# Chunked attention and a squared-ReLU feed-forward layer: where three blocks' transposes of x are done

## The chip, the cores and the metric

One core of a Trainium2 chip runs the kernel. The metric is the device time of one execution in microseconds (us); 283.85 us is the median of three executions before the change.

The engines are named as the profile names them: PE (TensorE: matrix products, and PEld, its weight loads), DVE (VectorE), ACT (ScalarE), POOL (GpSimd) and SP (SyncE, which here issues DMAs). Each engine has its own instruction queue, which it works off in the order in which the program put instructions in it.

## The reference

The inputs q, k and v have 8 batches, 8 heads, 576 positions and 64 elements a head. Attention stays inside chunks of 64 positions. Its output, 4608 rows of 512, goes through a feed-forward layer with 2048 hidden units:

```python
scores = scale * np.matmul(q_c, k_c.transpose(0, 1, 2, 4, 3))   # 64 x 64 per chunk and head
attn = softmax(scores)
x = matmul(attn, v_c)             # -> rows of 512
h = np.maximum(x @ w_in, 0.0)
return (h * h @ w_out).astype(np.float32)
```

## The kernel before

**Tiling.** A group is 256 rows (four chunks); there are 18. A block is two groups, 512 rows; there are 9, numbered 0 to 8. Groups 14 and 15 (block 7) consist of the four leftover chunks of four batches each; all others have four neighbouring chunks of one batch.

**What is done for a group g.** Its q and k are loaded by SP, cast to bf16 (`C`, on ACT or POOL) and transposed into `qkT` (`TD`, a DMA transpose on SP). `SC` (`scores`, L474) makes the scores in PSUM, and ACT takes the exponential `e` (L485). `AV` (`values`, L501) multiplies by v in two halves, `AV0` and `AV1`; after each half DVE takes a reciprocal (L435) and multiplies (L436), which gives half of `x`. `XT` (`transpose_x`) turns x into `xT`, the form that the feed-forward layer reads. It has two ways: eight PE transposes into one PSUM tile (L531) and a copy of 128x1024 out of it by ACT (L536), or one DMA transpose from SBUF to SBUF issued by SP (L526). `FIRST_DMA_X = 12` gives the DMA way to groups 12 to 17, which are blocks 6, 7 and 8.

**PSUM.** SC, each half of AV, and XT by PE each take a tile from `att_bank()`. In blocks 0 to 3 two tiles, `ps_att` and `ps_att2`, are given out in turn. From block 4 on there is `ps_att` alone. So such a step can write only when the reader of the tile's last content (ACT's exponential or copy, DVE's multiply) is done.

**The order is written by hand in slots.** While block j is worked on, attention for block j+1 and loads, casts and `qkT` for block j+2 are placed between its pieces.

Block 2: slots 0 to 15 follow the sixteen pieces of `ffn_in` (four products of 128x512 each, then a ReLU on ACT, L581, and a square into `gT`, L588). At slots 14 and 15 DVE is also given the sums of gT that the output stage needs (`g_sum`, L604): at 14 the first half of `d4`; at 15 the second half of d4, then d5, d3 and d2, seven additions. Slots 16 to 18 come with no work of the block. Slots 19 to 32 follow the fourteen half products of the output stage (`ffn_out`, L766), eight matrix products each. The seven products read, in this order: gT alone; d4; d5; d3; gT; gT; d2. They accumulate in two PSUM tiles, and after the second (slot 22), third and fourth, ACT copies a tile to `kept` (L823). The third product adds to the tile that the copy of slot 22 reads.

Blocks 4 to 8 use a fast form of the first product with seven smaller products, on four quarters ("ticks") of four slots. A slot s of such a block runs in this order: its `quad_step`s (L647: eight matrix products, or four in every fourth slot), what was placed at s - 0.5, half a product of the output stage of the block before (L766, eight matrix products; in block 4 in some slots only, and in blocks 5 to 8 at 0, 2, 3 and 5 to 15), and what was placed at s. From block 5's on, SC, AV0, AV1 and XT of the next block's two groups are placed by `S0`, `V0`, `V1` and `X0`. The four sums `e1` to `e4` of xT (`x_sums`, L604 `qk_st<-xT`), which the next block's first slots read, are placed at 13.5, 15, 17.5 and 18. e1 needs the first group's xT, e2 the second's. e1 is read in the next block's slot 0, e2 in its slot 2, e3 in its slot 3.

In the quad steps ACT copies one result (L683, L689, L692) or takes a ReLU (L703), DVE adds and clips (L655), and the squares go to ACT (L664), DVE and POOL (L666), some steps later.

Of the kernel before, what the change touches and what calls it, by code (L numbers as in the profile page):

```python
# [144 lines left out]
def kernel(  # L145
# [34 lines left out]


    FIRST_DMA_T = 4
    FIRST_DMA_X = 12
    QUADS = 4
    LEAD = 4

# [128 lines left out]
    def go(pieces):  # L315
        for f in pieces:
            f()
# [24 lines left out]
    def half_of(g):  # L342

        return g % 2 if g // 2 < QUADS else 1 - g % 2

    def x_tile(j):
        if j not in xTs:
            xTs[j] = att_pool.tile([128, BT // 128, n_dt, 128], BF16, name="xT", bufs=2)
        return xTs[j]
# [171 lines left out]
    def transpose_x(g):  # L521
        x = state.pop(("x", g))
        n = 2 * half_of(g)
        dst = x_tile(g // 2)[:, n:n + 2].rearrange("p t h q -> p (t h) q")
        if g >= FIRST_DMA_X:
            nc.sync.dma_start_transpose(out=dst, in_=x.rearrange("p t h a d -> p (t h a d)"))  # L526
            return
        psb = att_bank().bitcast(BF16)[:, 0:1024].rearrange("p (b q) -> p b q", q=128)
        for t in range(2):
            for hp in range(n_hp):  # L530
                nc.tensor.transpose(  # L531
                    out=psb[:, t * n_hp + hp, :],
                    in_=x[:, t, hp].rearrange("p a d -> p (a d)"),
                    identity=ident)
        copy = nc.vector.tensor_copy if g == blocks[1][0] else nc.scalar.copy
        copy(out=dst, in_=psb)  # L536
# [372 lines left out]
    def pieces(grps):  # L909
        for g in grps:  # L910
            yield from qk_pieces(g)
        for g in grps:
            yield from v_pieces(g)

    SC, AV, XT = scores, values, transpose_x
    TD = transpose_qk_dma
# [67 lines left out]
    for j in range(QUADS):  # L984
        grps, nxt, far = blocks[j], blocks[j + 1], blocks[j + 2]
        plan = {}

        def at(slot, f, *x):
            plan.setdefault(slot, []).append((f, x))

        if j == 0:
            loads, go_slots = pieces(far), range(17)
            at(28, summed(b11_p_b21, b11, b21))
            for slot, f in ((24, TA), (27, SC), (29, AV), (31, XT)):
                at(slot, f, nxt[0])
            at(31, TQ, nxt[1])
            at(31, summed(b22_m_b21, b22, b21, ALU.subtract))
            phases = [first_ffn_in, ffn_out_by_ft(0)]
        elif j == 1:
            loads, go_slots = itertools.chain(*map(qk_pieces, far)), range(26, 48)  # L1000
            for slot, f in ((1, TK), (4, SC), (7, AV), (12, XT)):
                at(slot, f, grps[1])
            for i, g in enumerate(nxt):
                for slot, f in ((16 + 4 * i, C), (21 + 4 * i, TD), (36 + i, SC), (38 + 2 * i, AV),
                                (41 + 2 * i, XT)):
                    at(slot, f, g)
            for i, g in enumerate(far):
                at(36 + 4 * i, C, g)
                at(42 + 3 * i, TD, g)
            at(2, summed(b12_p_b21, b12, b21))  # L1010
            at(12, summed(b11_m_b12, b11, b12, ALU.subtract))
            at(20, summed(b12_p_b22, b12, b22))
            out_j = ffn_out(1)
            for i in (20, 27, 29, 31):
                at(i, lambda: next(out_j)())
            phases = [ffn_in(1, [(0, 256, FT_ORDER), (256, 256, FT_ORDER)]), out_j]
        else:
            out_j = ffn_out(j)
            for i in (14, 15):
                at(i, lambda: next(out_j)())  # L1020
            phases = [ffn_in(j, [(0, BT, range(n_ft))])]
            if j == 2:
                loads, go_slots = itertools.chain(*map(v_pieces, nxt), pieces(far)), [
                    *range(16), *range(27, 36)]
                slots = {SC: (6, 9), AV: (11, 15), XT: (14, 24), C: (21, 26), TD: (25, 29)}
                for f in (C, TD):
                    for i, g in enumerate(far):
                        at(slots[f][i], f, g)
                phases.append(out_j)
            else:  # L1030
                loads, go_slots = pieces(far), range(11)
                for f, slots in ((C, (11, 13)), (TD, (13, 15))):
                    for i, g in enumerate(far):
                        at(slots[i], f, g)
                slots = {SC: (2, 4), AV: (7, 10), XT: (13, 15)}
            for f in (SC, AV, XT):
                for i, g in enumerate(nxt):
                    at(slots[f][i], f, g)
            if j == 2:
                for i, f in enumerate((summed(a21_p_a22, a21, a22),  # L1040
                                       summed(a12_m_a21, a12, a21, ALU.subtract),
                                       summed(a11_p_a21, a11, a21))):
                    at(1 + 2 * i, f)
        slot = 0
        for phase in phases:
            for _ in phase:
                if slot in go_slots:
                    for f in loads:
                        f()
                        break  # L1050
                for f, x in plan.get(slot, []):
                    f(*x)
                slot += 1
        assert all(x < slot for x in plan), (j, slot, sorted(plan))
        if j < QUADS - 1:
            go(loads)
# [19 lines left out]
    for j in range(QUADS, n_blk):  # L1076
        if j == QUADS:
            n = 14 - LEAD
            slots = [1 + 19 * i // n for i in range(n)]
            assert len(slots) == n  # L1080
        else:
            slots = [s for s in range(4, 20) if s % 16 not in NO_OUT]
            start = 3
        if j == QUADS:
            between = {}
            for n in (0, 1, 2, 3):
                between.setdefault(n, []).append((load, (1, loads)))
            for n in (2, 2, 2, 3):
                between.setdefault(n, []).append((x_sums, (QUADS, len([1 for z in between.values() for y in z if y[0] is x_sums]))))
            for f, x in between.get(0, []):  # L1090
                f(*x)
            for i in range(LEAD):
                next(out_j)
                tock()
                for f, x in between.get(i + 1, []):
                    f(*x)
        else:
            outs[j - 1] = ffn_out(j - 1)
            at(j, start, lambda j=j: next(outs[j - 1])())
        for s in slots:  # L1100
            plan.setdefault(("out", 16 * (j - QUADS) + s), []).append(outs[j - 1])

        if j + 1 < n_blk:
            S0, V0, V1, X0 = ((1.5, 3.5), (4.5, 7.5), (6, 9.5), (8.5, 11.5)) if j == QUADS else (
                (0.5, 7), (2, 8), (3.5, 9.5), (3.5, 10)) if is_whole(blocks[j + 1][0]) else (
                (3.5, 9), (5, 10), (7, 11.5), (7.5, 12))
            for i, g in enumerate(blocks[j + 1]):
                at(j, S0[i], SC, g)
                at(j, V0[i], AV0, g)
                at(j, V1[i], AV1, g)  # L1110
                at(j, X0[i], XT, g)
            if j + 2 == n_blk:
                at(j, 22, check_sums)
                at(j, 25.5, count_bad)
            for i, s in enumerate((13.5, 15, 17.5, 18)):
                at(j, s, x_sums, j + 1, i)
        if j == QUADS:
            for s in range(4):
                at(j, 4 * s + 2, w_sums_in_place, s)
            assert next(loads, None) is None  # L1120
        if j + 2 < n_blk:
            more = pieces(blocks[j + 2])
            if j == n_blk - 3:

                for s, n in ((0, 1), (1, 1), (2, 1), (3, 1), (4, 1), (5, 1), (10, 2), (12.5, 3),
                             (14, 1), (14.5, 1), (15, 1), (15.5, 1)):
                    at(j, s, load, n, more)
            else:
                for s in range(0, 16):
                    at(j, s, load, 1 if is_whole(blocks[j + 2][0]) else 2, more)  # L1130
            for i in range(2):
                at(j, (9, 13)[i], C, blocks[j + 2][i])
                at(j, ((9.5, 13.5) if j == n_blk - 3 else (12, 13.5))[i], TD, blocks[j + 2][i])
# [66 lines left out]
```

## Time and profile before

| What | us |
|---|---|
| runs before: median (lowest to highest of 3) | 283.85 (282.85 to 285.76) |
| the profiled execution's own time | 284.43 |
| its span, first to last instruction | 282.7 |
| PE busy | 267.3 (95%) |
| DVE busy | 199.3 (71%) |
| ACT busy | 166.2 (59%) |
| POOL busy | 93.5 (33%) |

The page's first part gives these shares. The chain of work that ended last is followed back from the last instruction to what released each step. The view of waits says for how long an engine sat idle before a line and what ended that. In the timeline a row is: start, duration, engine, line, operation, result and operands, count, and in square brackets the idle time before it with its releaser. The granted clock of PE was 1.000 throughout.

Where the blocks lie in this execution: block 2 from 81.4 to 112.4 us, block 3 to about 132, block 4 to about 155, block 5 to about 181, block 6 to 208, block 7 from 208.45. PE's idle time is 6.0 us in the first 20 us, 4.2 us in the last 16.7, and 5.1 us between.

### The profile page before, as it was taken

To read this page: it belongs to the slowest core of one execution; us is meant where nothing else is said; L and a number is where in the kernel's file an instruction comes from. 1 tells how busy PE (TensorE), PEld (TensorE's weight loads), DVE (VectorE), ACT (ScalarE), POOL (GpSimd) and SP (SyncE) were. 2 spreads that over 40 slices of the span, in tenths; PEclk is the share of its full clock that TensorE was granted. 3 is DMA by queue.
4 is the path that set the end of the run, shared out by engine and by line. 5 is a ranking of instruction groups with operands and counts; after the bars stand their busy time and mean duration, and the time that the engine had idled before them with its cause. 6 is when DMAs were issued, how large, how long until landed. Compare 5 with 4: busy or idle time off the path is not lost.

```text
span 282.7 us, 7975 instructions
## 1 busy us (share of the span) xinstructions
PE 267.3 (95%) x3288; PEld 204.7 (72%) x3291; DVE 199.3 (71%) x367; ACT 166.2 (59%) x296; POOL 93.5 (33%) x123
## 2 busy tenths in 40 slices
PE   2999999999999989999999999999988999999994
PEld 2774455788764478457879888888866888888883
DVE  1277515999438491499989997889739977994751
ACT  1537614794468845866678766475656664656330
POOL 2047842440350003151245234541703322431612
PEclk9999999999999999999999999999999999999999
DMA  7999999989999994999998997598999420220323
GB/s 221 255 339 392 379 306 277 334 184 163 303 188 234 240 199 102 268 257 187 242 231 181 176 220 198 118 217 224 219 186 228 101 72 4 82 67 9 79 71 114
DMA packets 135480, 55.61 MB, mean 197 GB/s; under 512 B 104272, under 2 KB 131152, under 8 KB 135440
## 3 DMA queue, kind: packets, MB, share of 16 engines
q1 hardware_dynamic: 132432, 45.76, 70.7%
q0 software_dynamic: 2864, 9.18, 10.3%
q8 instruction: 27, 0.44, 0.7%
q10 hardware_dynamic: 144, 0.13, 0.1%
q14 instruction: 13, 0.11, 0.1%
HBM read 36.70 MB, written 9.44 MB: 163 GB/s over the span
## 4 chain that ended last, share of the span: by engine, by line
PE 76%; DMA 10%; DVE 8%; ACT 2%; issue 1%; SPq 1%; DVEq 0%; ACTq 0%
PE ps_ffn L647 19%; PE ps_out L766 18%; PE ps_ffn L570 14%; PE ps_ffn L766 11%; PE ps_ffn L883 5%; DMA xT<-x 4%; DMA qk_st<-in_k_dram 4%; DVE w_st L604 2%; PE ps_att L474 2%; PE ps_att L501 2%; DVE gT L588 2%; DMA qkT<-qkb 2%; DVE x L436 2%; PE ps_ffn L426 1%; PE ps_att L531 1%
## 5 line engine op out<-in xcount | busy, mean ns | idle before, releaser
L570 PE MATMUL ps_ffn<-xT,w_in_bf 128*128 128x512 bf16 (+1 forms) x328 | 58.7, 333 | 0.3 <-DVE xT L536 0.2
L766 PEld LDWEIGHTS <-w_st 128*128 128x128 bf16 x512 | 49.0, 98 | 7.3 <-issue 0.8
L655 DVE CUSTOM_DVE_ANT_0 relu<-ps_ffn,w_st 128x512 f32<-128x512 f32 x60 | 39.3, 684 | 12.9 <-PE ps_ffn L647 11.9
L588 DVE TENSOR_TENSOR gT<-relu 128x256 bf16<-128x256 bf16 (+2 forms) x69 | 33.3, 512 | 20.1 <-ACT relu L581 19.9
L581 ACT ACTIVATE relu<-ps_ffn 128x256 bf16<-128x256 f32 (+2 forms) x82 | 39.9, 504 | 11.7 <-PE ps_ffn L570 10.3
L570 PEld LDWEIGHTS <-w_in_bf 128*128 128x128 bf16 x328 | 30.9, 98 | 21.6 <-DVE xT L536 0.4
L795 POOL DMA_DIRECT2D out_dram<-o_sb x27 | 19.8, 732 | 52.3 <-DVE o_sb L604 50.9
L647 PE MATMUL ps_ffn<-qk_st,w_in_bf 128*128 128x256 bf16 x240 | 35.3, 273 | 1.2 <-DVE qk_st L604 1.2
L647 PEld LDWEIGHTS <-w_in_bf 128*128 128x128 bf16 x320 | 30.6, 98 | 5.6 <-DVE qk_st L604 1.0
L766 PE MATMUL ps_out<-w_out_bf,w_st 128*128 128x256 bf16 x240 | 31.0, 273 | 0.1
L766 PEld LDWEIGHTS <-gT 128*128 128x128 bf16 x296 | 28.5, 98 | 3.4
L689 ACT ACTIVATE w_st<-ps_ffn 128x512 f32<-128x512 f32 x20 | 11.9, 597 | 26.8 <-PE ps_ffn L647 26.8
L436 DVE TENSOR_TENSOR x<-ps_att,recs 128x512 bf16<-128x512 f32 x36 | 24.9, 691 | 1.2
L647 PEld LDWEIGHTS <-qk_st 128*128 128x128 bf16 x240 | 22.6, 98 | 4.3 <-DVE qk_st L604 1.4
L485 ACT ACTIVATE e<-ps_att 128x1024 bf16<-128x1024 f32 x18 | 18.4, 1024 | 11.8 <-PE ps_att L474 11.8
L666 POOL TENSOR_TENSOR qk_st<-relu 128x512 bf16<-128x512 f32 x10 | 10.3, 1034 | 41.9 <-DVE relu L655 41.9
L647 PE MATMUL ps_ffn<-xT,qk_st 128*128 128x256 bf16 x160 | 23.9, 273 | 0.0
L666 POOL TENSOR_TENSOR gT<-relu 128x512 bf16<-128x512 f32 x10 | 10.3, 1033 | 39.5 <-DVE relu L655 35.8
L442 POOL CAST qkb<-qk_st 128x1024 bf16<-128x1024 f32 x12 | 13.5, 1124 | 14.1 <-DMA qk_st<-in_q_dram 14.1
L664 ACT ACTIVATE gT<-relu 128x512 bf16<-128x512 f32 x28 | 17.7, 633 | 0.0
L766 PE MATMUL ps_ffn<-w_out_bf,w_st 128*128 128x256 bf16 x144 | 17.5, 273 | 0.0
L445 POOL CAST qkb<-qk_st 128x1024 bf16<-128x1024 f32 x12 | 14.6, 1215 | 8.4 <-DMA qk_st<-in_k_dram 8.4
(91 smaller groups left out, 433.7 us busy)
## 6 DMA issues: line engine op xcount, KB each, us to landing
qk_st<-in_q_dram SPq DMA_DIRECT2D x16, 512.0 KB, 5.4
out_dram<-o_sb POOLq DMA_DIRECT2D x31, 256.0 KB, 4.3
qk_st<-in_k_dram SPq DMA_DIRECT2D x24, 256.0 KB, 5.3
ve_sb<-in_v_dram SPq DMA_DIRECT2D x32, 128.0 KB, 3.9
w_st<-in_moe_w_in_dram SPq DMA_DIRECT2D x8, 512.0 KB, 6.4
w_st<-in_moe_w_out_dram SPq DMA_DIRECT2D x8, 512.0 KB, 5.5
vo_sb<-in_v_dram SPq DMA_DIRECT2D x24, 128.0 KB, 3.3
qk_st<-in_k_dram SPq DMA_DIRECT2D x4, 512.0 KB, 5.8
```

Of the source, the lines that this page charges most:

```text
L436: nc.vector.tensor_tensor(out=x, in0=o[:, :, :, 0:D], in1=rec.to_broadcast([128, 2, n, D]), op=ALU.mult)
L445: copies[1](out=qkb[:, 1], in_=loaded(g, 1))
L485: nc.scalar.activation(out=e_out, in_=s_in, func=AF.Exp, scale=scale)
L570: nc.tensor.matmul(out=h[:, 0:n], lhsT=w_in_bf[:, dt, ft * 128:(ft + 1) * 128], rhs=xT[:, c // 128:(c + n) // 128, dt, :], start=(dt == 0) ...
L581: nc.scalar.activation(out=rl[:, 0:n], in_=h[:, 0:n], func=AF.Relu)
L588: nc.vector.tensor_tensor(out=dst, in0=src, in1=src, op=ALU.mult)
L647: nc.tensor.matmul(out=bank[:, f * GT:(f + 1) * GT], lhsT=a[:, dt, ft * 128:(ft + 1) * 128], rhs=b[:, :, dt, :], start=(first and f == 0 a ...
L655: nc.vector._custom_dve(TENSOR_ADD_SAT, out=out, in0=in0, in1=in1, s0=BIG, s1=0.0)
L664: engine.activation(out=dst, in_=r, func=AF.Square)
L666: engine.tensor_tensor(out=dst, in0=r, in1=r, op=ALU.mult)
L766: nc.tensor.matmul(out=out_ps, lhsT=lhsT, rhs=b[:, i, :], start=(first and i == 0 and (last or t == 0)), stop=(i == HF - 1), skip_group_ch ...
L795: dma.dma_start(out=out[t0:t0 + GT, col:col + HD].rearrange("(t p) d -> p t d", p=128), in_=o_sb.rearrange("p (t d) -> p t d", d=HD))
```

## The change

Three edits.

1. The DMA way of XT is given to blocks 6 and 8 by name. Groups 14 and 15 (block 7) so take the PE way: sixteen PE transposes and two ACT copies in place of two DMA transposes. For the attention of block 7, placed during block 6, the slots of the first group's XT go from 7.5 to 8.5, and those of the second group from 9, 10, 11.5 and 12 (SC, AV0, AV1, XT) to 9.5, 10.5, 12 and 13.5.
2. In block 2, AV of group 7 goes from slot 15 to 14, and XT of groups 6 and 7 from slots 14 and 24 to 22 and 28.
3. In block 4, XT of group 10 goes from 8.5 to 8.

```diff
-    FIRST_DMA_X = 12
+    X_BY_DMA = (6, 8)
...
-        if g >= FIRST_DMA_X:
+        if g // 2 in X_BY_DMA:
             nc.sync.dma_start_transpose(out=dst, in_=x.rearrange("p t h a d -> p (t h a d)"))
             return
...
-                slots = {SC: (6, 9), AV: (11, 15), XT: (14, 24), C: (21, 26), TD: (25, 29)}
+                slots = {SC: (6, 9), AV: (11, 14), XT: (22, 28), C: (21, 26), TD: (25, 29)}
...
-            S0, V0, V1, X0 = ((1.5, 3.5), (4.5, 7.5), (6, 9.5), (8.5, 11.5)) if j == QUADS else (
+            S0, V0, V1, X0 = ((1.5, 3.5), (4.5, 7.5), (6, 9.5), (8, 11.5)) if j == QUADS else (
                 (0.5, 7), (2, 8), (3.5, 9.5), (3.5, 10)) if is_whole(blocks[j + 1][0]) else (
-                (3.5, 9), (5, 10), (7, 11.5), (7.5, 12))
+                (3.5, 9.5), (5, 10.5), (7, 12), (8.5, 13.5))
```

## The prediction, made before the change was run

> **What bounds the kernel now.** I read the shares first, then the chain that ended last.
>
> ```profile
> PE 267.3 (95%) x3288; PEld 204.7 (72%) x3291; DVE 199.3 (71%) x367; ACT 166.2 (59%) x296; POOL 93.5 (33%) x123
> ...
> PE 76%; DMA 10%; DVE 8%; ACT 2%; issue 1%; SPq 1%; DVEq 0%; ACTq 0%
> ```
>
> PE is busy nearly all the time, so a stage has to give what PE idles in it, and work added to PE costs its length. Of 15.4 us idle, 5.1 lie between the first 20 and the last 16.7 us. The view of PE's waits says on whom:
>
> ```profile
> PE ps_ffn L647 <- DVE qk_st L604: 2.4, 3, 1.3
> PE ps_att L501 <- ACT xT L536: 0.9, 2, 0.7
> PE ps_ffn L766 <- ACT kept L823: 0.7, 1, 0.7
> ...
> PE ps_att L531 <- DVE x L436: 0.2, 1, 0.2
> ```
>
> (Total, times, longest.) The first row stands for the sums of block 7's x; the others lie mostly in block 2. The chain shows the two DMA transposes of block 7's x, and the timeline what follows each:
>
> ```profile
> 199.56 8.38 DMA xT<-x
> ...
> 208.55 3.77 DMA xT<-x
> ```
>
> ```profile
> 207.96 0.43 DVE L604 TENSOR_TENSOR qk_st<-xT 128x512 bf16<-128x512 bf16 x1 [1.83 <-DMA xT<-x]
> ...
> 208.45 0.61 PE L647 MATMUL ps_ffn<-qk_st,w_in_bf 128*128 128x256 bf16 x4 [0.77 <-DVE qk_st L604]
> ...
> 212.42 0.42 DVE L604 TENSOR_TENSOR qk_st<-qk_st,xT 128x512 bf16<-128x512 bf16 x1 [3.43 <-DMA xT<-x]
> ...
> 212.90 0.61 PE L647 MATMUL ps_ffn<-qk_st,qk_st 128*128 128x256 bf16 x4 [1.28 <-DVE qk_st L604]
> ...
> 215.62 0.60 PE L647 MATMUL ps_ffn<-qk_st,w_in_bf 128*128 128x256 bf16 x4 [0.40 <-DVE qk_st L604]
> ```
>
> The transfers land late, DVE stands in front of e1 and e2, and PE behind DVE.
>
> **Edit 1 (block 6).** *Removed:* 0.77 + 1.28 + 0.40 = 2.45 us of PE waits. The first group's x is done at 194.4; PE reaches slot 8.5 at 195.83; ACT, idle from 194.97 to 197.30, copies (1.01 us) until 197.5, ten us ahead of e1. The second group's copy ends near 208.5 in my layout, e2's addition (0.42) near 209; PE needs it at 212.4.
>
> *Added on PE:* block 4's sets of eight transposes hold PE from 145.89 to 146.35 and from 150.06 to 150.51, so two sets cost 0.92. Nothing hides them.
>
> *Added wait:* the second group's SC now comes behind slot 10's quad steps, AV0 behind slot 11's. Counted from slot 10's first product, SC ends at 0.89 + 0.37 = 1.26, and PE stands at AV0 after an output half (0.96) and four products (0.44) more, at 2.66. ACT has three instructions ahead of the exponential that used to run behind it:
>
> ```profile
> 197.30 1.02 ACT L485 ACTIVATE e<-ps_att 128x1024 bf16<-128x1024 f32 x1 [2.34 <-PE ps_att L474]
> 198.22 0.59 ACT L689 ACTIVATE w_st<-ps_ffn 128x512 f32<-128x512 f32 x1
> 198.70 0.63 ACT L664 ACTIVATE gT<-relu 128x512 bf16<-128x512 f32 x1
> 199.22 0.60 ACT L703 ACTIVATE relu<-ps_ffn 128x512 f32<-128x512 f32 x1
> ```
>
> They start 0.5 apart; the first can start 0.63 after slot 10's first product (in slot 14: 204.46 and 205.09). So the exponential runs from 2.11 to 3.13, and PE waits some 0.5 us; behind AV0 on PE stand output products, which nobody else holds up. Bounds: 0 if the ACT work is out of the way, 1.02 if a whole exponential is waited for. I take 0.5.
>
> *On SP:* two issues (2.27 and 1.24 us) go. The cast that the next `qkT` transpose of SP needs ends at 200.6, and that transpose was issued at 201.92, behind the removed one; it and the v loads come earlier. The last v for AV0 of group 16 landed at 211.2 + 3.1 = 214.3, PE came at 214.90 and will come near 213.9; SP's head start of over 2 us covers that.
>
> Sum of edit 1: -2.45 + 0.92 + 0.5 = -1.0 (bounds -1.5 and -0.5).
>
> **Edit 2 (block 2).** PE's three waits there:
>
> ```profile
> 98.24 0.22 PE L501 MATMUL ps_att<-ve_sb,e 64*64 64x65 bf16 x2 [0.70 <-ACT xT L536]
> ...
> 102.84 1.91 PE L766 MATMUL ps_ffn<-w_out_sum,w_st 128*128 128x256 bf16 x16 [0.67 <-ACT kept L823]
> ...
> 105.22 0.40 PE L531 MATMUL ps_att<-ident,x 128*128 128x128 bf16 x4 [0.25 <-DVE x L436]
> ```
>
> Before, from the end of the last `ffn_in` piece (97.2) to block 3's first product (112.4) lie AV of group 7 with its wait, 1.29; seven products, 12.3; the `kept` wait, 0.67; group 7's XT with its wait, 0.87.
>
> After: AV takes the place of group 6's XT ahead of the last piece, at about the same PE time; its half of the PSUM tile is free when DVE's x ends at 95.96, as it was for XT. The 1.29 goes. Group 6's XT (0.46) fits into the `kept` wait (0.67), which stays as a whole. Group 7's XT finds its x long done: 0.45, so 0.42 goes.
>
> A new wait comes by DVE. Its 1.49 us idle before the last square now takes AV's two reciprocals and multiplies (94.20 to 95.96: 1.76). The second half of d4 ends at 100.1 instead of 99.87, while PE reaches the product that reads it 1.29 sooner: four matrix products after 98.96, at 99.4. PE waits 0.7. d5 (101.4), d3 (102.6) and d2 (103.8) still come before PE needs them (102.2, 103.9, 109.6). ACT's casts of group 9 and group 7's copy end near 109, ahead of block 3; the `qkT` transpose behind the casts, issued at 109.90, comes 1.5 us sooner, into a stretch in which the DMA engines are nearly empty (share 0.03 from 108 to 110 us).
>
> Sum of edit 2: -1.29 - 0.42 + 0.7 = -1.0. Bounds: -1.7 without DVE's wait; 0 if DVE, 97% busy in block 3, gives it all back.
>
> **Edit 3 (block 4).** AV0 of group 11 uses the same single `ps_att`, one output half earlier:
>
> ```profile
> 145.15 0.69 DVE L436 TENSOR_TENSOR x<-ps_att,recs 128x512 bf16<-128x512 f32 x1
> ...
> 145.89 0.62 PE L531 MATMUL ps_att<-ident,x 128*128 128x128 bf16 x8
> ```
>
> DVE releases the tile at 145.84. Slot 8 ends on PE at 144.97, so the transposes, moved there, hold up PE by 0.9 us, and slot 9's products (0.92), which filled this time, stand behind them. What comes back: AV1 of group 11 waited 0.23 for XT's copy, and two hand-overs of some 0.07. PE reaches AV1 at 148.15 instead of 147.62: **+0.5**, bounds -0.2 (DVE far ahead) and +0.9.
>
> **Sum:** -1.0 - 1.0 + 0.5 = -1.5 us; 284.43 - 1.5 = 282.9 against the profiled execution. The median of the runs lies 0.58 below that execution, so I forecast 283.85 - 1.5 = **282.3 us** (-0.5%). About 1% is what a measurement of this kernel can tell from no change.
>
> **Skill and trace on the transposes.** Two sets of eight took 0.46 us each here. The Trainium skill (TensorE: Matmul & The Clock Gate, Part 4: PE-mode transpose) puts one 128x128 bf16 transpose at about 275 ns inside a kernel and says that latency dominates it; an estimate by that page is 4.4 us for sixteen, and a sum of +2.0. The trace does not agree: its rows of L531 last 219 ns, but start some 55 ns apart.
>
> **Rivals.**
> - *The added waits stay out* (17%). ACT and DVE drain sooner than I lay out: edits 1 and 2 at their lower bounds, edit 3 at 0: -3.2, 280.6 us. For it: the L664 square can fall before slot 10. Against: DVE's order in block 2 and the tile in block 4 are plain in the rows.
> - *What is won ahead of block 6 is given back there* (13%). SC of group 14 at 187.29 follows a `qkT` transfer issued at 182.18 that took 5.07; PEld waited 0.42 for it. SP issues almost without a gap from 176.79. If that chain can't move up, edits 2 and 3 cancel out and -1.0 is left: 282.8. Against: SP stood waiting for x at 176.4 to 176.79 and for POOL's cast until 155.09, both paced by PE.
> - *Slower: `ps_att` hand-overs in block 6* (12%). XT by PE adds a writer and ACT a reader to the one tile; each step now waits for the last reader: XT on DVE, SC on ACT's copy, AV1 and XT on DVE again. If four of these cost the 0.70 that block 2's case cost, +2.8: 285.1. It ends slower than before once they sum to 1.5. Against: the layout leaves each 0.7 to 1.6 us.
> - *Slower: transposes that don't overlap* (2%). At 219 ns in a row sixteen take 3.5 instead of 0.92: 284.9.
> - *The stall is not the DMA's* (3%): DVE or the next transfer is late anyway, only costs remain: -1.0 + 0.5 + 1.4, 284.8. Against: DVE idled 1.83 and 3.43 in front of just these two sums.
>
> The forecast has 53%, with its own range 281.4 to 283.3.
>
> **Numbers.** Range 280.5 to 284.7: from the first rival down to most of the slower cases. Faster by over 1% is below 281.0: most of the first rival and a tail, 18%. Slower by over 1% is above 286.7: only if hand-overs cost more than priced, 8%. Within 1%: 74%.
>
> **What would show it.** No wait of DVE for `xT<-x` near 208, PE's row L647 <- DVE `qk_st` gone; a wait of about 0.5 for `e` at group 15's AV0; in block 2 a wait of about 0.7 of L766 on DVE's `w_st` and none of L501 on the copy; block 3 starting near 111.4; a wait of about 0.9 of L531 on DVE's x in block 4. The forecast is wrong if PE's idle time between 20 and 266 us falls by less than 1 us or by over 4.

## The result and the profile after

The changed kernel takes 283.56 us (median of 22 runs); the kernel before, run beside it, 285.31 us (22 runs, the three of the table above among them). The ratio is **0.9952, interval 0.993 to 0.9974**: faster by 0.5%, or 1.4 us, and clear of no change; the two medians lie 1.75 us apart. Here and below a ratio leaves out runs that took over 1.5% longer than the fastest of the same kernel, while a median holds all runs. The forecast was 282.3 us, with a range of 280.5 to 284.7 and most of the chance on "within 1%". The profiled execution took 284.07 us, with a span of 282.3.

The page of the kernel after, the shares of busy time and of the chain that ended last:

```profile
PE 268.1 (95%) x3304; PEld 205.6 (73%) x3307; DVE 201.1 (71%) x367; ACT 167.9 (59%) x298; POOL 91.9 (33%) x123
...
PE 81%; DVE 11%; ACT 3%; DMA 2%; issue 1%; SPq 0%; ACTq 0%; DVEq 0%
```

DMA's share of the chain went from 10% to 2%. PE is busy 0.8 us longer, with the sixteen transposes that it now does. DVE's share of the chain rose from 8% to 11%, by 8 us: 5 of them in block 4, where the transposes now stand behind DVE's x, and most of the rest in the first 60 us, where no edit reaches. In block 2 it is about as large as before.

PE's waits after (line, what ended the wait: total us, times, longest):

```profile
PE ps_att L531 <- DVE x L436: 1.0, 2, 0.8
PE ps_ffn L570 <- DVE xT L517: 1.0, 1, 1.0
PE ps_att L501 <- ACT e L485: 0.5, 2, 0.4
PE ps_ffn L766 <- DVE w_st L604: 0.5, 1, 0.5
PE ps_out L766 <- DVE w_st L604: 0.4, 1, 0.4
...
PE ps_ffn L766 <- ACT kept L823: 0.2, 1, 0.2
```

The list leaves out the opening's row of 4.7 us, which leads it before and after. The row that came next before (L647 on `qk_st`, 2.4 us) is gone. So are the 0.7 us of L501 on the copy of `xT`. Four of the six rows are what the edits left in their place, L531, L501, L766 on `w_st` into `ps_ffn`, and `kept`. The other two lie near 20 us and in block 3, where no edit reaches. The timeline has them with their places:

```profile
100.83 0.69 DVE L604 TENSOR_TENSOR w_st<-gT 128x1024 bf16<-128x1024 bf16 x1
...
101.58 1.48 PE L766 MATMUL ps_ffn<-w_out_bf,w_st 128*128 128x256 bf16 x12 [0.53 <-DVE w_st L604]
...
103.73 1.91 PE L766 MATMUL ps_ffn<-w_out_sum,w_st 128*128 128x256 bf16 x16 [0.23 <-ACT kept L823]
...
146.73 0.62 PE L531 MATMUL ps_att<-ident,x 128*128 128x128 bf16 x8 [0.77 <-DVE x L436]
...
200.49 1.02 ACT L485 ACTIVATE e<-ps_att 128x1024 bf16<-128x1024 f32 x1
...
201.57 0.22 PE L501 MATMUL ps_att<-ve_sb,e 64*64 64x65 bf16 x2 [0.38 <-ACT e L485]
...
207.44 0.61 PE L531 MATMUL ps_att<-ident,x 128*128 128x128 bf16 x8
207.89 1.04 PE L766 MATMUL ps_out<-w_out_sum,gT 128*128 128x256 bf16 x8
...
208.16 0.41 DVE L604 TENSOR_TENSOR qk_st<-xT 128x512 bf16<-128x512 bf16 x1
```

From the top: d4's second half ends at 101.52 and PE starts behind it (block 2); the rest of the `kept` wait; the transposes of group 10 behind DVE's x (block 4); AV0 of group 15 behind its exponential (block 6). Then the second group's transposes start without a wait and are followed 0.45 us later by the next products. In the last row DVE makes e1, without the wait for `xT` of 1.83 us that it had before.

**The same work, stage by stage.** Since the two kernels run the same instructions outside the edits, the time between two of them can be compared. The marks are a ReLU of block 1 (L581, near 62 us) and the first L689 of each block from 4 on. "Before" is the profiled execution and four more that are told of below; "after" is the profiled execution and two more (*whole*, *whole_b*).

| Stretch, us | before, five executions | after, three | difference of the means |
|---|---|---|---|
| start to block 1's mark | 61.4, 62.0, 62.3, 62.4, 62.2 | 62.9, 62.2, 62.5 | +0.5 |
| to block 4's (edit 2) | 73.9, 74.3, 74.0, 75.1, 74.3 | 73.2, 73.3, 73.2 | -1.1 |
| block 4 (edit 3) | 23.3 in all | 23.9 in all | +0.6 |
| block 5 | 25.1 in all | 25.1 in all | 0 |
| blocks 6 and 7 (edit 1) | 56.8, 55.9, 56.3, 55.3, 57.2 | 55.1, 55.1, 55.1 | -1.2 |
| the rest | 42.1 in all | 42.1 in all | 0 |

The edits' three rows sum to -1.7 us; with the opening, which no edit touches and which differs from execution to execution, -1.2. The runs say -1.4. Other profiles agree: *edits12* and *edits12_b* (edits 1 and 2, experiments 1 and 4) take 73.2 to 73.3 us to block 4's mark and 55.1 to 55.2 in blocks 6 and 7, while *edit3* and *before_td10*, which have neither edit, take 74.3 to 74.7 and 56.3 to 57.6.

### The profile page after: what moved, and what is told of

It is laid out like the page before. It is cut to its first block, busy times and chain, and to the rows that moved or that the text cites. A ratio compares the mean times of both kernels' runs of the same rounds, so it can differ in the third digit from the quotient of the medians.

```text
span 282.3 us, 8007 instructions
## 1 busy us (share of the span) xinstructions
PE 268.1 (95%) x3304; PEld 205.6 (73%) x3307; DVE 201.1 (71%) x367; ACT 167.9 (59%) x298; POOL 91.9 (33%) x123
## 4 chain that ended last, share of the span: by engine, by line
PE 81%; DVE 11%; ACT 3%; DMA 2%; issue 1%; SPq 0%; ACTq 0%; DVEq 0%
PE ps_ffn L647 21%; PE ps_out L766 20%; PE ps_ffn L570 15%; PE ps_ffn L766 13%; PE ps_ffn L883 5%; DVE x L436 3%; DVE gT L588 3%; PE ps_att L474 2%; PE ps_att L501 2%; DMA qk_st<-in_k_dram 2%; DVE w_st L604 2%; PE ps_att L531 1%; PE ps_ffn L426 1%; PE ps_ffn L393 1%; DVE relu L655 1%
## 5 line engine op out<-in xcount | busy, mean ns | idle before, releaser
L766 PEld LDWEIGHTS <-w_st 128*128 128x128 bf16 x512 | 48.9, 98 | 8.0 <-DVE w_st L604 1.7
L581 ACT ACTIVATE relu<-ps_ffn 128x256 bf16<-128x256 f32 (+2 forms) x82 | 39.9, 503 | 12.7 <-PE ps_ffn L570 11.2
L588 DVE TENSOR_TENSOR gT<-relu 128x256 bf16<-128x256 bf16 (+2 forms) x69 | 34.3, 529 | 17.3 <-ACT relu L581 16.9
L647 PE MATMUL ps_ffn<-qk_st,w_in_bf 128*128 128x256 bf16 x240 | 35.3, 273 | 0.0
L647 PEld LDWEIGHTS <-w_in_bf 128*128 128x128 bf16 x320 | 30.7, 98 | 4.0 <-issue 0.2
L766 PE MATMUL ps_out<-w_out_bf,w_st 128*128 128x256 bf16 x240 | 31.0, 273 | 0.4 <-DVE w_st L604 0.4
L766 PEld LDWEIGHTS <-gT 128*128 128x128 bf16 x296 | 28.5, 98 | 3.5
L689 ACT ACTIVATE w_st<-ps_ffn 128x512 f32<-128x512 f32 x20 | 11.9, 597 | 26.7 <-PE ps_ffn L647 26.7
L647 PEld LDWEIGHTS <-qk_st 128*128 128x128 bf16 x240 | 22.6, 98 | 2.9
L647 PE MATMUL ps_ffn<-xT,qk_st 128*128 128x256 bf16 x160 | 23.9, 273 | 0.0
L766 PE MATMUL ps_ffn<-w_out_bf,w_st 128*128 128x256 bf16 x144 | 17.7, 273 | 0.5 <-DVE w_st L604 0.5
L664 ACT ACTIVATE gT<-relu 128x512 bf16<-128x512 f32 x28 | 17.7, 632 | 0.0
L604 DVE TENSOR_TENSOR w_st<-gT,w_st 128x1024 bf16<-128x1024 bf16 x26 | 17.5, 706 | 0.0
L445 POOL CAST qkb<-qk_st 128x1024 bf16<-128x1024 f32 x12 | 13.9, 1156 | 10.2 <-DMA qk_st<-in_k_dram 10.2
```

The lines of the kernel that those rows point to most:

```text
L581: nc.scalar.activation(out=rl[:, 0:n], in_=h[:, 0:n], func=AF.Relu)
L588: nc.vector.tensor_tensor(out=dst, in0=src, in1=src, op=ALU.mult)
L604: nc.vector.tensor_tensor(out=out, in0=in0, in1=in1, op=op)
L647: nc.tensor.matmul(out=bank[:, f * GT:(f + 1) * GT], lhsT=a[:, dt, ft * 128:(ft + 1) * 128], rhs=b[:, :, dt, :], start=(first and f == 0 a ...
L664: engine.activation(out=dst, in_=r, func=AF.Square)
L766: nc.tensor.matmul(out=out_ps, lhsT=lhsT, rhs=b[:, i, :], start=(first and i == 0 and (last or t == 0)), stop=(i == HF - 1), skip_group_ch ...
```

## The experiments

**1. Each edit alone, and two together.** Theory: the three edits are separate terms, of -1.0, -1.0 and +0.5. Rival: the gain is all edit 1's, or edits 2 and 3 are given back at a transfer. The four kernels ran on one chip, beside a median before of 286.81.

*edit1*, edit 1 alone:

```diff
-    FIRST_DMA_X = 12
+    X_BY_DMA = (6, 8)
...
-        if g >= FIRST_DMA_X:
+        if g // 2 in X_BY_DMA:
...
-                (3.5, 9), (5, 10), (7, 11.5), (7.5, 12))
+                (3.5, 9.5), (5, 10.5), (7, 12), (8.5, 13.5))
```

> Edit 1 alone. My theory: the three PE waits on the sums of x (2.45 us) go, two sets of transposes (0.92) and a wait of 0.4 to 0.5 for the exponential at group 15's AV0 come; against the profile of before, PE's products shift by +1.3 to +1.4 across block 6 and by -2.5 to -2.9 after it, net -1.0 to -1.6, ratio about 0.995. Rival (the stall is not the DMA's): PE still waits for DVE near the first sums, net 0 or more, ratio 1.000 or above.

Measured: 284.1 us, ratio 0.9881 (0.9816 to 0.9945). That is more than -1.0; the last point of the section on the forecast comes back to it. Its timeline:

```profile
191.88 0.45 PE L474 MATMUL ps_att<-qkT 64*64 64x64 bf16 x32 [2.54 <-DMA qkT<-qkb]
...
204.94 0.22 PE L501 MATMUL ps_att<-ve_sb,e 64*64 64x65 bf16 x2 [0.38 <-ACT e L485]
```

The sums' waits are gone and the 0.38 of the exponential is there, as in the whole change. The first row is the wait that the rival "given back" named: SC of group 14, behind its `qkT` transfer. It is most of what makes this execution (287.43) longer than the median. It stands at a place that comes before edit 1's slots, so edit 1 has not caused it.

*edit2*, edit 2 alone:

```diff
-                slots = {SC: (6, 9), AV: (11, 15), XT: (14, 24), C: (21, 26), TD: (25, 29)}
+                slots = {SC: (6, 9), AV: (11, 14), XT: (22, 28), C: (21, 26), TD: (25, 29)}
```

> Edit 2 alone. My theory: PE's products are some 1.0 us earlier at block 3's first product, with a wait of about 0.5 on DVE's second half of d4; about 0.3 of it is given back at block 3's own d4 (DVE is behind there). Net about -0.7 at block 4, ratio about 0.997. Rival (given back at the qkT transfer for group 14): the shift is gone by the first products after 188 us, ratio 1.000.

Measured: 285.06 us, ratio 0.9949 (0.9918 to 0.998): a gain of 1.5 us (0.6 to 2.4), which holds the 1.0 of the forecast. Its profiled execution was the longest of the thirteen (289.58 us), with waits of 1.49 us for a load of v and of 1.76 for a `qkT` transfer, both at places that edit 2 does not move, so the gain is not read from it.

*edit3*, edit 3 alone:

```diff
-            S0, V0, V1, X0 = ((1.5, 3.5), (4.5, 7.5), (6, 9.5), (8.5, 11.5)) if j == QUADS else (
+            S0, V0, V1, X0 = ((1.5, 3.5), (4.5, 7.5), (6, 9.5), (8, 11.5)) if j == QUADS else (
```

> Edit 3 alone. My theory: a wait of 0.8 to 0.9 of the transposes on DVE's x of group 11, the later wait for the copy (0.2) gone, PE later by 0.5 from slot 10 of block 4 on, ratio about 1.002. Rival: DVE is ahead enough, no wait, ratio 1.000 or a little below.

Measured: 287.16 us, ratio 0.9989 (0.9949 to 1.0029), which can't tell +0.5 from nothing. Its timeline can:

```profile
147.38 0.62 PE L531 MATMUL ps_att<-ident,x 128*128 128x128 bf16 x8 [0.77 <-DVE x L436]
```

This is the same 0.77 as in the whole change, and block 4 takes 23.9 us here, against 23.3.

*edits12*, edits 1 and 2 as above, without edit 3:

> Edits 1 and 2 without edit 3. My theory: the sum, -1.7 to -2.3 us, 0.5 us faster than the whole change; ratio about 0.993. Rival (edit 3 costs nothing in the end): the ratio of the whole change, 0.995, or above.

Measured: 283.03 us, ratio 0.9846 (0.9788 to 0.9904). Its timeline shows block 2 as in the whole change, and block 4 as before, with only the wait for the copy that edit 3 removes:

```profile
101.54 1.48 PE L766 MATMUL ps_ffn<-w_out_bf,w_st 128*128 128x256 bf16 x12 [0.53 <-DVE w_st L604]
...
103.70 1.91 PE L766 MATMUL ps_ffn<-w_out_sum,w_st 128*128 128x256 bf16 x16 [0.23 <-ACT kept L823]
...
148.53 0.22 PE L501 MATMUL ps_att<-ve_sb,e 64*64 64x65 bf16 x2 [0.23 <-ACT xT L536]
```

What follows: edits 1 and 2 both gain, each alone. Edit 3 takes away a wait of 0.23 us and makes one of 0.77.

**2. The way or the slots.** Theory: the gain of edit 1 comes from the PE way, and the slots keep its new waits small. Rival: the slots bring it, and the way is a cost. On another chip, beside a median before of 286.54. First *whole*, the changed kernel again:

> The whole change again, beside the others of this call. My theory: 0.5 us slower than edits 1 and 2 without edit 3, so a ratio of 0.987 to 0.995 on a chip where those two have 0.985 to 0.993; a wait of 0.8 of the transposes on DVE's x in block 4. Rival (edit 3 costs nothing): the same ratio as without it.

Measured: 283.43 us, ratio 0.989 (0.9847 to 0.9932), with waits of 0.53, 0.23, 0.77 and 0.38 us at the four places shown above. 

*way_only*, the PE way for block 7 in the old slots:

```diff
-    FIRST_DMA_X = 12
+    X_BY_DMA = (6, 8)
...
-        if g >= FIRST_DMA_X:
+        if g // 2 in X_BY_DMA:
```

> Block 7's x by PE, but in the slots of before. My theory: the three waits on the sums go as in edit 1; the transposes wait for DVE's x, about 0.3 for the first group and 0.6 for the second, and there is no wait for the exponential: 0.5 us slower than edit 1 alone, still faster than before, net -0.5 to -1.0. Rival (the slots are what brings the gain): no gain.

Measured: 286.02 us, ratio 0.9988 (0.9951 to 1.0024). Its timeline:

```profile
160.41 0.45 PE L474 MATMUL ps_att<-qkT 64*64 64x64 bf16 x32 [1.74 <-DMA qkT<-qkb]
...
197.50 0.62 PE L531 MATMUL ps_att<-ident,x 128*128 128x128 bf16 x8 [0.21 <-DVE x L436]
...
207.28 0.62 PE L531 MATMUL ps_att<-ident,x 128*128 128x128 bf16 x8 [0.52 <-DVE x L436]
```

In the old slots the single `ps_att` costs 0.21 and 0.52 us, where PE reaches the transposes before DVE has read the tile. With the 0.92 of the transposes that is 1.65 of the 2.3 that the sums' waits cost on the average of seven profiles (experiment 5); what is left is too small for these runs. Its blocks 6 and 7 took 55.7 us in the one profile, 0.6 below the mean of the five executions before.

*slots_only*, the new slots with the DMA way:

```diff
-                (3.5, 9), (5, 10), (7, 11.5), (7.5, 12))
+                (3.5, 9.5), (5, 10.5), (7, 12), (8.5, 13.5))
```

> Edit 1's slots, but block 7's x still by DMA. My theory: the second DMA transpose is issued behind three more v loads, lands 2 to 3 us later, and PE's wait for e2 grows by as much; with a wait of 0.4 for the exponential on top, +2 to +3.5 us, ratio 1.007 to 1.012. Rival (the slots bring the gain, not the way): a ratio below 1.

Measured: 289.25 us, ratio 1.0079 (1.004 to 1.0119), slower. Its timeline:

```profile
190.84 0.45 PE L474 MATMUL ps_att<-qkT 64*64 64x64 bf16 x32 [1.74 <-DMA qkT<-qkb]
...
203.46 0.22 PE L501 MATMUL ps_att<-ve_sb,e 64*64 64x65 bf16 x2 [0.38 <-ACT e L485]
...
216.65 0.43 DVE L604 TENSOR_TENSOR qk_st<-qk_st,xT 128x512 bf16<-128x512 bf16 x1 [5.39 <-DMA xT<-x]
217.13 0.61 PE L647 MATMUL ps_ffn<-qk_st,qk_st 128*128 128x256 bf16 x4 [2.46 <-DVE qk_st L604]
```

The second transfer took 3.62 us from its issue (212.93) to its landing, no longer than before (3.77); it comes late because it is issued late. DVE idles 5.39 us in front of e2, and PE 2.46 behind it, where it waited 1.28 before. But there is no wait for e1 here, and the sums' waits add up to 2.86, only 0.6 more than the average before; with the 0.38 of the exponential that is about 1 of the 2.3 us that the runs lose, and the rest is not shown. So the slots alone are a loss, the way alone gains nothing that the runs can tell, and the two together gain.

**3. A better set of slots.** Both kernels of this kind leave out edit 3 and keep the PE way and edit 2. *tuned* also moves the second group's SC in block 6 back to 9, where its exponential is in time, and the first group's XT to 8:

```diff
-                (3.5, 9), (5, 10), (7, 11.5), (7.5, 12))
+                (3.5, 9), (5, 10.5), (7, 12), (8, 13.5))
```

> Edits 1 and 2 without edit 3, and in block 6 the first group's XT at 8 instead of 8.5 and the second group's SC at 9 instead of 9.5. My theory: the exponential is ahead of slot 10's three ACT instructions again, the wait of 0.4 at group 15's AV0 goes, nothing else comes; 0.4 us faster than edits 1 and 2 alone, 0.9 faster than the whole change. Rival (ps_att hand-overs): a wait of SC on the copy of xT or of XT on x, 0.3 or more, takes its place.

Measured: 282.51 us, ratio 0.9865 (0.9823 to 0.9906). That is 0.9 below *whole* on the same chip, as the theory has it, though the two intervals overlap. AV0 of group 15 doesn't wait in its profile, and blocks 6 and 7 take 54.6 us. In block 2 this execution had a wait of AV of group 6 for its v, at slot 11, which no edit moves. Of the others only the long execution of *edit2* has more than 0.25 us there:

```profile
PE ps_att L501 <- DMA vo_sb<-in_v_dram: 1.2, 1, 1.2
```

**4. Are the `qkT` transfers why the kernel before scatters?** Four profiles above have a wait of 1.7 to 2.5 us for a `qkT` transfer (*edit1*, *edit2*, *way_only*, *slots_only*). Theory: such waits make the medians before of 286.5 to 286.8, above the profiled 284.43, and an earlier issue removes them. *before_td10* is the kernel before with the first group's transfer in blocks 4 and 5 issued two slots earlier; *tuned_td10* is *tuned* with the same edit:

```diff
-                at(j, ((9.5, 13.5) if j == n_blk - 3 else (12, 13.5))[i], TD, blocks[j + 2][i])
+                at(j, ((9.5, 13.5) if j == n_blk - 3 else (10, 13.5))[i], TD, blocks[j + 2][i])
```

> Before, with the first group's qkT transfer in blocks 4 and 5 at slot 10 instead of 12 alone. My theory: the qkT transfer for group 14 lands ahead of its use by 3 us or more, so the waits of 1.7 to 2.5 us that come in some executions go; the median falls by 0.5 to 1.5 us. Rival (the spread of before comes from other places, such as the landing of xT): the same median.

Measured: 286.7 us, ratio 0.9999 (0.9964 to 1.0034), beside a median of 286.56. The theory falls, as far as this one issue goes.

> Edits 1 and 2, the exponential of group 15 ahead (first XT at 8, second SC at 9), and in blocks 4 and 5 the first group's qkT transfer at slot 10 instead of 12. My theory: PE's waits of 1.7 to 2.5 us for a qkT transfer at 160 and 190, which the profiles of some executions show, go, because the transfer is issued 2 to 4 us sooner; 0.9 us faster than the whole change in the undisturbed runs, and a narrower spread. Rival: the v loads, now behind that transfer, come late, and AV of group 12 or 14 waits for them instead.

Measured: **282.35 us**, ratio 0.9832 (0.9792 to 0.9871), with all six runs between 281.54 and 282.47. It has the lowest median of the kernels run, but its interval overlaps those of *edits12*, *edits12_b* and *tuned*. PE's waits in it, from 0.7 down:

```profile
PE ps_ffn L393 <- DMA qk_st<-in_q_dram: 4.7, 1, 4.7
PE ps_out L766 <- DVE w_st L604: 0.7, 1, 0.7
PE ps_ffn L393 <- DMA qk_st<-in_k_dram: 0.4, 1, 0.4
```

The first and third belong to the opening.

On the same chip, the whole change and edits 1 and 2 again:

> The whole change, for comparison inside this call. My theory: a ratio of 0.989 to 0.995.

> Edits 1 and 2 without edit 3, beside the whole change. My theory: 0.5 us faster than the whole change, ratio lower by 0.002. Rival (edit 3 costs nothing in the end): the same median within 0.2 us.

Measured: *whole_b* 283.85 us, ratio 0.9887 (0.9841 to 0.9933); *edits12_b* 282.69 us, ratio 0.9862 (0.9821 to 0.9903). The kernel without edit 3 is some 1.1 us below the one with it. The two ratios' intervals overlap, but the sign is that of the 0.6 us in the table of stages.

**5. Was the profiled execution before a typical one?** The forecast rests on one execution and three runs. Four more executions of the kernel before, unchanged, each with a profile. Theory A: block 7's transfers of x land later in others; theory B: the difference is waits for `qkT`; theory C: it lies elsewhere.

> Before, unchanged, one more profiled execution. Theory A (the landing of the DMA transposes of x varies): PE's waits on the sums of block 7's x add up to more than the 2.45 us of the first profile, 3 to 5 us, in most executions. Theory B (qkT transfers): the waits of 1.7 to 2.5 us of SC for a qkT transfer are there in most executions, and the sums' waits stay near 2.5. Theory C (elsewhere, such as the opening): neither.

> As for the first of these looks: A, waits on the sums of 3 to 5 us; B, a qkT wait of 1.7 us or more with sums near 2.5; C, neither.

> As for the first of these looks: A, waits on the sums of 3 to 5 us; B, a qkT wait of 1.7 us or more with sums near 2.5; C, neither.

> As for the first of these looks: A, waits on the sums of 3 to 5 us; B, a qkT wait of 1.7 us or more with sums near 2.5; C, neither.

| Execution of before | time, us | waits for the sums of block 7's x, us |
|---|---|---|
| the profile shown above | 284.43 | 0.77 + 1.28 + 0.40 = 2.45 |
| *look1* | 284.53 | 0 + 1.23 + 0.40 = 1.63 |
| *look2* | 284.88 | 0.51 + 1.22 + 0.40 = 2.13 |
| *look3* | 285.13 | 0 + 0.89 + 0.40 = 1.29 |
| *look4* | 286.02 | 1.24 + 1.43 + 0.40 = 3.07 |

The rows of *look4*, the longest:

```profile
209.93 0.61 PE L647 MATMUL ps_ffn<-qk_st,w_in_bf 128*128 128x256 bf16 x4 [1.24 <-DVE qk_st L604]
...
214.53 0.61 PE L647 MATMUL ps_ffn<-qk_st,qk_st 128*128 128x256 bf16 x4 [1.43 <-DVE qk_st L604]
...
217.25 0.60 PE L647 MATMUL ps_ffn<-qk_st,w_in_bf 128*128 128x256 bf16 x4 [0.40 <-DVE qk_st L604]
```

The wait is no constant: with *before_td10* (2.04) and *edit3* (3.46), seven profiles have 1.29 to 3.46 us of it, 2.3 on the average, so 2.45 was a fair size. Theory A does not explain the level: three of the other four wait less than the first profile and are longer. Nor does theory B: no wait for `qkT` above 0.3 us is in any of the four. What they have more is ahead of block 4. Block 4's first L689 starts at 135.3 us in the first profile and at 136.2 to 137.5 in the other four. So theory C holds for these: the first profile lay at the fast end because of its first half.

## Why the prediction was right or wrong

**The sum was right in the measurement that it was made for.** Forecast -1.5 us; the ratio says -1.4 (0.7 to 2.0), the stages of the edits -1.7. That the two sizes lie so close is in part luck: in experiments 1 to 4 the same change gained about 3 us (the last point of this section).

**Edit 1: right.** Forecast -1.0, measured -1.2 in blocks 6 and 7. Its terms: the sums' waits went as a whole; eight transposes hold PE for 0.45 us (0.46 forecast); AV0 waits 0.38 for the exponential (0.5). In the trace ACT runs three instructions (L689, L664, L703) from 199.00 on and the exponential from 200.49, which is the order that the forecast laid out. The Trainium skill's 275 ns (TensorE: Matmul & The Clock Gate, Part 4: PE-mode transpose) is the figure of one transpose inside a kernel; eight in a row at that price would be 2.2 us, an estimate by that page. The second set of eight, at 207.44, held PE for 0.45 us, like the sets in the rows of before: in a row they overlap, and the figure of one is not the price of each.

**Edit 2: right.** Forecast -1.0, measured -1.1 up to block 4's mark. Block 3 starts at 112.91 us and not near 111.4, because the opening of this execution is 1.5 us longer; counted from block 1's mark it starts 1.1 us earlier than before. Block 2's wait of 0.70 for the copy is gone; the wait for DVE's half of d4 came, 0.53 instead of 0.7; of the `kept` wait 0.23 is left, which with group 6's transposes of 0.46 makes up the old 0.67. The wait of 0.43 at 132.39, in block 3, isn't edit 2's doing: *look1*, *look3*, *look4*, *before_td10* and *edit3*, all without edit 2, have 0.44 to 0.56 there. One reading behind its bound was wrong: DVE is 97% busy in the last 12 us of block 3, from 120 on, and 74% in the whole block.

**Edit 3: right in size and sign.** Forecast +0.5, from a wait of 0.9; measured +0.6, from one of 0.77. It is the part of the change that costs, and the kernel without it was the faster one on the same chip (282.69 against 283.85).

**The level was wrong.** The step "The median of the runs lies 0.58 below that execution" took three runs for the kernel. Over 22 runs the median is 285.31, 1.46 above those three and 0.88 above the profiled execution instead of 0.58 below. So the forecast of 282.3 lies 1.26 below the 283.56 that was measured, nearly as much as the change itself; from the right level it would have been 285.31 - 1.5 = 283.8. The four further executions of experiment 5 show the same: all are longer than the profiled execution.

**What could be told apart was wrong, and with it the chances: this is the step that failed.** The sentence "About 1% is what a measurement of this kernel can tell from no change" turned a forecast of -0.5% into 74% for no difference. It was taken from three runs, which spread over 1%. But 22 against 22 give an interval of 0.22% to either side, and the 0.5% measured is a gain clear of it. The forecast had the sign and the size of a change that this resolves, and its chances called it none. The range has a slip of its own: it is said to reach down to most of the slower cases and ends at 284.7, while these cases were priced at 284.8, 284.9 and 285.1.

**PE's idle time** between 20 and 266 us fell from 5.17 to 3.71, by 1.46 us. The sum asked for 2.4 (the 1.5, and the 0.92 that PE works longer). Most of the difference is the two waits that this execution had and the one before lacked: 0.43 in block 3, and 0.48 of the 0.98 for DVE's `xT` (L517), which ended at 20.48 us.

**The rivals.** *The added waits stay out*: no, all three came. *Given back at the `qkT` transfer*: not in the three profiles of the whole change, but the wait exists, at group 14 in *edit1* and *slots_only*, and at block 5's first SC in *way_only* and *edit2*. *`ps_att` hand-overs*: in block 6 real in the old slots (0.21 and 0.52), absent in the new. *Transposes that don't overlap* and *the stall is not the DMA's*: fallen, by the rows at 207.44 and by the sums that no longer wait.

**What stays open.** On the two chips of experiments 1 to 4 the whole change gained 1.1% (0.989, 0.9887) and not 0.5%, and *edit1* alone more than its terms. The kernel before ran there at 286.5 to 286.8, and no profile of such a run was taken. The nearest is *edit3* (287.3 us), the kernel before but for the 0.6 us in block 4: its blocks 6 and 7 took 57.6 us and its sums' waits were 3.46, the longest on record. So a longer stall behind the transfers of x may be a part of it, but *before_td10*, profiled on the same chip at 284.61, had 2.04, and two executions don't show it. The `qkT` waits of 1.7 to 2.5 us are another candidate: four kernels with only a part of edits 1 and 2 had one, and none of the seven profiles with both. But the seven profiles of the kernel before, *before_td10* and *edit3* have none above 0.3 either, and moving one issue changed nothing, so this is not shown.

## What to carry to other kernels

Where PE is busy 95% of the time and stalls behind a transfer between on-chip buffers, doing the step on PE can pay: here its own cost was 0.92 us and a new wait of 0.38, the stall 1.3 to 3.5. It needs slots in which the one PSUM tile that it uses has just been read; in the old slots the same edit gained nothing that the runs could tell. Before moving a step ahead by half a slot, look up when the last reader of its tile ends; half a slot too early cost 0.6 us. Take the base from many runs and more than one profile: a median of three was 1.5 us off, as much as the whole change.

## What the runs showed that was not expected

- DMA transposes of x, all of one size, landed 3.0 to 8.4 us after their issue within one execution of *slots_only* (median 4.0); once block 7's two were gone, the other four of the profile after landed in 3.7 to 4.4.
- The DMA transposes of `qkT`, all of one size, landed in 4.4 to 7.7 us in the profile after and 4.2 to 8.0 in *edit1*; group 14's landed 4.4 us after its issue in the one and 7.4 in the other, and PE waited for it 0 and 2.54 us.
- The opening, up to the mark in block 1, differs by up to 1.5 us between executions (61.4 to 62.9), as much as the change is worth.
